# Where in a partition TensorE's streamed operands lie, against its weights: new offsets for two expert layers

## The chip, the core and the metric

One core of one Trainium2 chip runs the whole program. The metric is the device time of one execution in microseconds (us); the kernel before takes 991.43 us (median of 3 runs, 991.33 to 991.97). The engines are TensorE (PE in the rows, its weight loads PEld), VectorE (DVE), ScalarE (ACT), GpSimd (POOL) and SyncE (SP), which issues the DMAs. SBUF is the memory on the chip that operands are read from; it has 128 partitions, and an address here is the byte within a partition. PSUM, in banks of 512 floats per partition, takes the sums of TensorE.

## The reference, cut to what matters

```
x = attention(q, k, v, M_prev, z_prev, beta)      # 4 x 8 heads, 576 tokens of 64, causal, plus a memory term
x = x as [2304 tokens, 512]
h = x @ w_in            # 512 -> 2048
g = s * max(h, 0)**2 + b
x = g @ w_out           # 2048 -> 512          (layer 1)
h = x @ w_in2
g = max(h, 0) + alpha * min(h, 0)
return g @ w_out2       #                      (layer 2)
```

All of it is float32. The two layers hold most of the multiplications.

## The kernel before

**Matmuls of the layers.** A float32 matrix is split in a high and a low part (float32r), and a product is three matmuls: weight high by data high, weight high by data low, weight low by data high (in `g2` the order of the last two differs). Weights are the stationary operand, loaded by 128 x 128; the data is the moving operand, streamed through them, of 512 or 256 columns. Every matmul has its own weight load, which runs while the matmul before it streams.

**Stages.** Layer 1 takes its 2304 tokens in one block of 512 and seven of 256; layer 2 in four of 512 and one of 256 (`BLOCKS`). For each block and each of 16 slices f of the hidden dimension, `g1` (lines 923 to 957) makes 12 matmuls (4 slices d of the model dimension, three each, lines 932 to 934) from X into one PSUM bank; ScalarE and VectorE turn the result into G (layer 1: Relu at line 946, Square at 947, high part at 954, low part at 955; layer 2: lines 949, 952, 954, 955); `g2` (lines 959 to 980) makes 12 matmuls from G (lines 973 to 975) into the output's banks. The g2 of slice f stands behind the g1 of slice f + 1, so that TensorE has work while G is made. In layer 1 block 6 of `BLOCKS` (`ONES`) G has two further columns of ones, so its matmuls in g2 have 258 columns. Layer 1's output is written in halves of two banks (`y_of`, but for the blocks `WIDE`), layer 2's in four banks.

**Order.** `Plan.order` (lines 134 to 283) places all operations on the engines at build time by estimated durations, which depend on the number of columns (`t_r`, line 286), due times and free buffers; addresses don't enter. The attention of batches 0 to 3 is interleaved with layer 1 up to about 423 us of the span; then come the rest of layer 1 (to about 584 us) and layer 2.

**Where operands lie.** Tiles lie in the partition in the order in which they are made (lines 331 to 375, the weights `wt` 0 to 11 behind the last of them), each begun at a multiple of 32 bytes:
- `lead`, 64 bytes; `room` 12 to 15, 8192 bytes each, later the weights `wt` 12 to 15; `pool` 30720 and `poolx` 17920, multiples of 256. `xr2`, the X of layer 2, takes the place of `poolx`.
- `xr`, 16512 bytes (64.5 x 256), the X of layer 1.
- `gr`, 4608 bytes (18 x 256), then `gr2`, 4096: the G of both layers. `gr` has four buffers of 256 columns (2 x lo + j, j alternating with the slices f in layer 1) with a pitch of 1152 bytes (4.5 x 256), or two of 512 columns.
- small tiles (`gt`, `vsc`, `allone`, `mz`, `ident`, `mask` and so on) and `tail`, 96 bytes; together with the half in `xr` they bring `wt` 0 to the residue mod 256 that `room` 12 has (in the built program 2240 and 116928 bytes, both 192 mod 256; `xr` begins at 83648, also 192; `gr` at 100160 and `gr2` at 104768, both 64).
- `cut` (line 353) gives operand number k of n columns; those under 512 columns lie 64 bytes (`HALF`, 16 floats) further. `g_of` (line 907) does the same for `gr2`.

```
x = k * (step or n) + (HALF if n < NBIG else 0)
return t[:, x:x + n]
```

In layer 1 `gj` alternates 0 and 1 (0 for the block of 512), in layer 2 it alternates 0 and 2, where 2 stands for `gr2` (line 941). `xs` says which X buffer a block uses.

Of the kernel before, what the change touches and what calls it, by code (L numbers as in the profile page):

```python
# [6 lines left out]
F32 = mybir.dt.float32  # L7
F32R = mybir.dt.float32r
# [13 lines left out]
NBIG, NB = 512, 256  # L22

SCRATCH = 2048
TAIL = 24
HALF = 16
PITCH = NB + 2 * HALF

WIDE, ONES = (0, 6, 7), 6
KD = DM // 128  # L30
# [284 lines left out]
def build(tc, kp, vd, qp, mzd, beta8, sb2, win1, wout1, win2, wout2, alpha, outT):  # L315
# [8 lines left out]
    with tc.tile_pool(name="sb", bufs=1) as sb, tc.tile_pool(  # L324
        name="ps", bufs=1, space=bass.MemoryType.PSUM
# [2 lines left out]
        y1 = dr.tile([128, KD, NT], F32, name="y1")  # L328


        sb.tile([128, HALF], F32, name="lead")
        room = [sb.tile([128, 3 * GW], F32, name=f"room{f}", tag=f"wt{f}") if f >= KF - XF else None for f in range(KF)]
        made = {}

# [6 lines left out]
        poolx = sb.tile([128, XS * GW], F32, name="poolx", tag="poolx")  # L341

        def xr2():
            if "xr2" not in made:
                made["xr2"] = sb.tile([128, 2 * KD * NBIG + HALF], F32R, name="xr2", tag="poolx")
            return made["xr2"]

        xr_ = sb.tile([128, 4 * KD * NB + 2 * HALF], F32R, name="xr")
        gr_ = sb.tile([128, 4 * PITCH], F32R, name="gr")
        gr2 = sb.tile([128, 2, NBIG], F32R, name="gr2")  # L350
        gt_ = sb.tile([128, 2 * NB], F32, name="gt")

        def cut(t, n, k, step=None):

            x = k * (step or n) + (HALF if n < NBIG else 0)
            return t[:, x:x + n]

        vsc = sb.tile([128, 2, 6], F32, name="vsc")
# [15 lines left out]
        bcs = sb.tile([128, KD], F32, name="bcs")  # L374
        sb.tile([128, TAIL], F32, name="tail")

# [516 lines left out]
        def x_of(n, xs, lo, d):  # L893

            if xs == 2:
                return cut(xr2(), n, KD * lo + d)
            if n == NBIG:
                return cut(xr_, n, KD * lo + d)
            return cut(xr_, n, 2 * KD * xs + KD * lo + d, NB)
# [7 lines left out]
        def g_of(n, lo, j, extra=0):  # L907

            if j == 2:
                x = HALF if n < NBIG else 0  # L910
                return gr2[:, lo, x:x + n]
            if n == NBIG:
                return cut(gr_, n, lo)
            return cut(gr_, n + extra, 2 * lo + j, PITCH)

# [7 lines left out]
        def g1(layer, n, xs, f):  # L923
# [17 lines left out]
            gj = 2 * (cm["g"] % 2) if layer == 2 else 0 if n == NBIG else cm["g"] % 2  # L941
            cm["g"] += 1
            t_, G_h, G_l = t_of(n, gj), g_of(n, 0, gj), g_of(n, 1, gj)
            tk = ("gt", gj)
            if layer == 1:
# [13 lines left out]
        def g2(layer, blk, n, f, gj):  # L959
            extra = 2 if (layer, blk) == (1, ONES) else 0  # L960
            G_h, G_l = g_of(n, 0, gj, extra), g_of(n, 1, gj, extra)
            if f == 0:
                yslot.clear()
                if layer == 1 and blk in WIDE:
                    yslot.update({d: Bank([4 + d]) for d in (2, 3)})
            for d in range(KD):
                yk, Y = y_of(layer, blk, d)

                first = f == 0 and (layer == 2 or blk in WIDE or d % 2 == 0)

                def mm(d=d, Y=Y, first=first):
                    W_h, W_l = (wt(f, 1, lo)[:, d * 128:(d + 1) * 128] for lo in range(2))
                    T.matmul(Y, W_h, G_h, start=first, stop=False, skip_group_check=True)  # L973
                    T.matmul(Y, W_l, G_h, start=False, stop=False, skip_group_check=True)  # L974
                    T.matmul(Y, W_h, G_l, start=False, stop=False, skip_group_check=True)  # L975

                op("PE", 3 * t_r(n), mm, r=wkeys("wo", f) + [("gh", gj), ("gl", gj)],
                   w=[yk, ("g2", f)] + ([(yslot[d], "y")] if d in yslot else []),
                   prio=MOE + cm["m"] + (1.5 if layer == 1 and n == NBIG else 0))
            cm["m"] += 1  # L980

        def ones():


            for j in range(2):
                A.copy(out=g_of(NB, 0, j, 2)[:, NB:], in_=one)
                A.activation(out=g_of(NB, 1, j, 2)[:, NB:], in_=one, func=AF.Copy, scale=0.0)
# [165 lines left out]
```

## Time and profile before

| | |
|---|---|
| median of 3 runs | 991.43 us |
| the profiled execution | 990.51 us |
| its span, first to last instruction | 988.4 us |
| TensorE busy, of the span | 972.3 us (98%) |
| weight loads busy | 832.5 us (84%) |
| VectorE, ScalarE busy | 602.7 us (61%), 470.3 us (48%) |
| granted clock of TensorE, mean | 0.999 |

The profile records each instruction's start and duration. Matmuls overlap in the records, since the end of one is modelled, so the sum of durations says little; how fast TensorE goes is read from the distance of one start to the next. The timeline's starts are in us with two decimals, so that a distance over twelve matmuls is good to about 1 ns each.

### The profile page before, as it was taken

Reading aid. Unit: us, or ns where it says so; the run is one execution under the profiler, and the core shown is the slowest. Engines: PE = TensorE matmul, PEld = TensorE weight load, DVE = VectorE, ACT = ScalarE, POOL = GpSimd, SP = SyncE. Lnnn points to the kernel's source line nnn. Section 1 sums busy time; section 2 is a strip of 40 time slices with the busy share of each in tenths; the row PEclk is TensorE's granted clock in tenths of the full one; section 3 lists DMA queues with packets and bytes.
Section 4 is the critical chain, followed back from the end, with each engine's and each line's share of the span. In section 5 each row is a group of like instructions: output and inputs, shape, how many; then the busy total and the mean of one; then the engine's idle time right before and its main releaser. Section 6 shows DMA issues by size and latency. Waiting matters only on the chain.

```text
span 988.4 us, 18001 instructions
## 1 busy us (share of the span) xinstructions
PE 972.3 (98%) x7068; PEld 832.5 (84%) x7068; DVE 602.7 (61%) x1471; ACT 470.3 (48%) x1183; POOL 5.3 (1%) x29
## 2 busy tenths in 40 slices
PE   7999999999999999999999999999999999999998
PEld 5777777788888888999999998888888888888898
DVE  7999998677776766442122999945334433534354
ACT  7877766787777777644454653212112111211111
POOL 1000000000000000000000000000000000000000
PEclk9999999999999999999999999999999999999999
DMA  5359955475667545451000755402000100100010
GB/s 175 100 167 244 244 180 154 103 165 112 150 129 153 142 107 114 102 173 44 1 23 20 219 163 163 152 1 86 1 1 14 61 1 1 43 1 0 1 44 22
DMA packets 114692, 93.22 MB, mean 94 GB/s; under 512 B 83376, under 2 KB 94640, under 8 KB 114608
## 3 DMA queue, kind: packets, MB, share of 16 engines
q1 hardware_dynamic: 114608, 92.08, 34.6%
q8 instruction: 55, 0.90, 0.4%
q14 instruction: 29, 0.24, 0.1%
HBM read 59.29 MB, written 13.11 MB: 73 GB/s over the span
## 4 chain that ended last, share of the span: by engine, by line
PE 91%; DVE 4%; ACT 4%; issue 1%; DMA 0%; SPq 0%; ACTq 0%
PE yb L973 14%; PE yb L975 13%; PE yb L974 13%; PE hb L932 9%; PE hb L934 8%; PE hb L933 8%; PE sp L933 3%; PE sp L932 3%; PE sp L934 3%; PE ob L775 2%; PE ob L933 2%; PE ob L934 2%; PE ob L932 2%; PE yb L775 2%; PE sp L775 2%; PE sp L679 1%
## 5 line engine op out<-in xcount | busy, mean ns | idle before, releaser
L973 PE MATMUL yb<-gr,wt 128*128 128x256 f32 (+2 forms) x832 | 272.2, 327 | 0.7 <-ACT gr L954 0.5
L975 PE MATMUL yb<-gr,wt 128*128 128x256 f32 (+2 forms) x832 | 270.1, 325 | 0.0
L974 PE MATMUL yb<-gr,wt 128*128 128x256 f32 (+2 forms) x832 | 269.2, 324 | 0.0
L932 PE MATMUL hb<-xr,wt 128*128 128x256 f32 (+1 forms) x592 | 184.3, 311 | 5.3 <-ACT gt L946 3.7
L934 PE MATMUL hb<-xr,wt 128*128 128x256 f32 (+1 forms) x592 | 179.6, 303 | 0.3 <-DVE wt L882 0.3
L933 PE MATMUL hb<-xr,wt 128*128 128x256 f32 (+1 forms) x592 | 179.6, 303 | 0.0
L973 PEld LDWEIGHTS yb<-gr,wt 128*128 128x128 f32 x832 | 156.4, 188 | 18.0 <-issue 2.5
L975 PEld LDWEIGHTS yb<-gr,wt 128*128 128x128 f32 x832 | 156.6, 188 | 15.2 <-DVE gr L955 0.6
L974 PEld LDWEIGHTS yb<-gr,wt 128*128 128x128 f32 x832 | 156.3, 188 | 14.0
L955 DVE TENSOR_TENSOR gr<-gt,gr 128x256 fp32r<-128x256 f32 (+1 forms) x168 | 83.9, 499 | 129.8 <-ACT gr L954 129.1
L954 ACT CAST gr<-gt 128x256 fp32r<-128x256 f32 (+1 forms) x168 | 78.3, 466 | 146.3 <-DVE gt L952 139.1
L932 PEld LDWEIGHTS hb<-xr,wt 128*128 128x128 f32 x592 | 111.2, 188 | 18.5 <-ACT gt L946 5.9
L934 PEld LDWEIGHTS hb<-xr,wt 128*128 128x128 f32 x592 | 111.0, 188 | 6.0 <-DVE wt L882 0.7
L933 PEld LDWEIGHTS hb<-xr,wt 128*128 128x128 f32 x592 | 111.2, 188 | 4.7
L946 ACT ACTIVATE gt<-hb 128x256 f32<-128x256 f32 (+1 forms) x128 | 52.4, 410 | 102.7 <-PE hb L934 102.1
L954 ACT CAST gr<-mz 128x512 fp32r<-128x512 f32 (+1 forms) x40 | 23.1, 578 | 156.3 <-DVE mz L952 153.6
L933 PE MATMUL sp<-xr,wt 128*128 128x512 f32 (+1 forms) x160 | 58.9, 368 | 0.0
L932 PE MATMUL sp<-xr,wt 128*128 128x512 f32 (+1 forms) x160 | 58.9, 368 | 0.0
L934 PE MATMUL sp<-xr,wt 128*128 128x512 f32 (+1 forms) x160 | 58.9, 368 | 0.0
L947 ACT ACTIVATE gt<-gt 128x256 f32<-128x256 f32 (+1 forms) x128 | 56.8, 444 | 2.6
L955 DVE TENSOR_TENSOR gr<-mz,gr 128x512 fp32r<-128x512 f32 (+1 forms) x40 | 25.5, 638 | 25.0 <-ACT gr L954 25.0
L949 DVE TENSOR_SCALAR mz<-ob,alv 128x512 f32<-128x512 f32 (+1 forms) x20 | 13.9, 697 | 38.9 <-PE ob L934 38.9
(343 smaller groups left out, 1481.9 us busy)
## 6 DMA issues: line engine op xcount, KB each, us to landing
pool<-wout SPq DMA_DIRECT2D x18, 512.0 KB, 4.4
pool<-win SPq DMA_DIRECT2D x16, 512.0 KB, 4.3
room<-wout SPq DMA_DIRECT2D x14, 512.0 KB, 3.9
room<-win SPq DMA_DIRECT2D x13, 512.0 KB, 4.2
pool<-y SPq DMA_DIRECT2D x18, 256.0 KB, 4.3
out_t<-pool SPq DMA_DIRECT2D x16, 256.0 KB, 2.1
y<-pool SPq DMA_DIRECT2D x22, 128.0 KB, 1.8
pool<-kp SPq DMA_DIRECT2D x9, 288.0 KB, 4.1
```

The costliest lines, as they stand in the source:

```text
L775: T.matmul(bank_at(bk)[rows, x:x + n], half(sqp, odd, q0, nq), half(sk, odd, k0, n), start=True, stop=True, skip_group_check=True)
L932: T.matmul(H_, W_h, X_h, start=(d == 0), stop=False)
L933: T.matmul(H_, W_h, X_l, start=False, stop=False)
L934: T.matmul(H_, W_l, X_h, start=False, stop=(d == KD - 1))
L946: op("ACT", t_act(n, 50), lambda: A.activation(out=t_, in_=H_, func=AF.Relu), r=[hk, "gr"], w=[tk], prio=-1)
L947: op("ACT", t_act(n), lambda: A.activation(out=t_, in_=t_, func=AF.Square), w=[tk], prio=-1)
L949: op("DVE", t_dve(n, 1.04, 60), lambda: V.tensor_scalar(out=t_, in0=H_, scalar1=0.0, scalar2=alv[:, f:f + 1], op0=ALU.min, op1=ALU.mult), ...
L954: op("ACT", t_act(n), lambda: A.copy(out=G_h, in_=t_), r=[tk], w=[("gh", gj)], prio=-1)
L955: op("DVE", t_dve(n), lambda: V.tensor_tensor(out=G_l, in0=t_, in1=G_h.bitcast(F32), op=ALU.subtract), r=[tk, ("gh", gj)], w=[("gl", gj)], ...
L973: T.matmul(Y, W_h, G_h, start=first, stop=False, skip_group_check=True)
L974: T.matmul(Y, W_l, G_h, start=False, stop=False, skip_group_check=True)
L975: T.matmul(Y, W_h, G_l, start=False, stop=False, skip_group_check=True)
```

## The change

Operands of fewer than 512 columns begin 192 bytes (`SKEW`, 48 floats) further instead of 64; the pitch of the four buffers in `gr` is 1280 bytes (5 x 256) instead of 1152; `xr` has 16640 bytes (65 x 256) instead of 16512, `tail` 224 instead of 96. So `gr` and `gr2` begin at the residue mod 256 of the weights, and `wt` 0 keeps it. `gr2` and the small tiles begin 640 bytes further on, `gr` 128, `wt` 0 to 11 768.

```diff
-TAIL = 24
-HALF = 16
-PITCH = NB + 2 * HALF
+TAIL = 56
+SKEW = 48
+PITCH = 320
...
-        sb.tile([128, HALF], F32, name="lead")
+        sb.tile([128, 16], F32, name="lead")
...
-                made["xr2"] = sb.tile([128, 2 * KD * NBIG + HALF], F32R, name="xr2", tag="poolx")
+                made["xr2"] = sb.tile([128, 2 * KD * NBIG + SKEW], F32R, name="xr2", tag="poolx")
...
-        xr_ = sb.tile([128, 4 * KD * NB + 2 * HALF], F32R, name="xr")
+        xr_ = sb.tile([128, 4 * KD * NB + 64], F32R, name="xr")
...
-            x = k * (step or n) + (HALF if n < NBIG else 0)
+            x = k * (step or n) + (SKEW if n < NBIG else 0)
...
-                x = HALF if n < NBIG else 0
+                x = SKEW if n < NBIG else 0
```

## Rows read from the trace of the kernel before

**Rows 1.** The page: busy time by engine; the costliest group of instructions.
```profile
PE 972.3 (98%) x7068; PEld 832.5 (84%) x7068; DVE 602.7 (61%) x1471; ACT 470.3 (48%) x1183; POOL 5.3 (1%) x29
...
L973 PE MATMUL yb<-gr,wt 128*128 128x256 f32 (+2 forms) x832 | 272.2, 327 | 0.7 <-ACT gr L954 0.5
```

**Rows 2.** The page: the chain of waits that ended last, by engine.
```profile
PE 91%; DVE 4%; ACT 4%; issue 1%; DMA 0%; SPq 0%; ACTq 0%
```

**Rows 3.** Windows: length, busy us and instructions by engine, granted clock, DMA.
```profile
core 0: us, PE busy (x) PEld busy (x) DVE busy (x) ACT busy (x) POOL busy (x), PEclk, DMA share, GB/s
64.00:184.00 120.00, 117.03 (x685) 87.12 (x686) 110.60 (x274) 83.25 (x189) 0.41 (x2) 1.00 0.72 196
184.00:423.00 239.00, 237.80 (x2569) 210.29 (x2569) 161.20 (x512) 181.98 (x509) 2.04 (x10) 1.00 0.57 129
423.00:584.00 161.00, 160.53 (x1378) 159.63 (x1371) 70.73 (x149) 82.41 (x203) 0.00 (x0) 1.00 0.30 94
600.00:900.00 300.00, 300.00 (x1305) 244.51 (x1304) 151.83 (x231) 51.12 (x85) 0.00 (x0) 1.00 0.12 37
```

**Rows 4.** Timeline of TensorE in layer 2 (start, duration, both us): 512 columns.
```profile
723.35 0.40 PE L973 MATMUL yb<-gr,wt 128*128 128x512 f32 x1
...
726.14 0.39 PE L932 MATMUL sp<-xr,wt 128*128 128x512 f32 x1
...
726.84 0.39 PE L932 MATMUL sp<-xr,wt 128*128 128x512 f32 x1
...
728.88 0.40 PE L973 MATMUL yb<-gr,wt 128*128 128x512 f32 x1
```

**Rows 5.** Timeline of TensorE in layer 1: 256 columns, G at 64, X, G at 192.
```profile
471.50 0.28 PE L973 MATMUL yb<-gr,wt 128*128 128x256 f32 x1
...
472.92 0.28 PE L932 MATMUL hb<-xr,wt 128*128 128x256 f32 x1
...
474.33 0.28 PE L973 MATMUL yb<-gr,wt 128*128 128x256 f32 x1
...
474.68 0.28 PE L973 MATMUL yb<-gr,wt 128*128 128x256 f32 x1
...
475.70 0.28 PE L932 MATMUL hb<-xr,wt 128*128 128x256 f32 x1
```

**Rows 6.** Timeline of TensorE in layer 2's last block: 256 columns, G at 192.
```profile
953.08 0.28 PE L973 MATMUL yb<-gr,wt 128*128 128x256 f32 x1
...
954.49 0.28 PE L932 MATMUL sp<-xr,wt 128*128 128x256 f32 x1
```

**Rows 7.** Timeline of TensorE in block ONES: G of 258 columns, X of 256.
```profile
502.84 0.28 PE L973 MATMUL yb<-gr,wt 128*128 128x258 f32 x1
...
504.29 0.28 PE L932 MATMUL hb<-xr,wt 128*128 128x256 f32 x1
...
505.70 0.28 PE L973 MATMUL yb<-gr,wt 128*128 128x258 f32 x1
...
507.13 0.28 PE L932 MATMUL hb<-xr,wt 128*128 128x256 f32 x1
...
508.49 0.28 PE L973 MATMUL yb<-gr,wt 128*128 128x258 f32 x1
```

**Rows 8.** Timeline of TensorE: two G runs at 192 behind a break.
```profile
250.36 0.28 PE L975 MATMUL yb<-gr,wt 128*128 128x256 f32 x1
...
250.70 0.28 PE L975 MATMUL yb<-gr,wt 128*128 128x256 f32 x1
...
423.55 0.28 PE L974 MATMUL yb<-gr,wt 128*128 128x256 f32 x1
...
424.84 0.28 PE L932 MATMUL hb<-xr,wt 128*128 128x256 f32 x1
```

**Rows 9.** Timeline of TensorE: a G run at 192 behind X of 512.
```profile
584.49 0.28 PE L973 MATMUL yb<-gr,wt 128*128 128x256 f32 x1
...
585.17 0.39 PE L932 MATMUL hb<-xr,wt 128*128 128x512 f32 x1
```

## The prediction

> **What bounds the kernel.** First the page's busy shares, then its chain of waits: TensorE is busy for 98% of the span, and 91% of the chain that ended last is its own matmuls [rows 1, 2]. Then the windows by stage: from 184 us on TensorE is busy in 237.80 of 239, 160.53 of 161 and 300 of 300 us, while VectorE and ScalarE have room [rows 3]. Before 184 us it is less clear: 64 to 184 has VectorE at 110.60 of 120. At the clock the windows show 1.00, the 2.4 GHz level, so no clock is to be won back. L973, first to need a new G, stood idle 0.7 us in 832 times [rows 1]. So the end is set by how soon one matmul follows the other, and the durations of the groups do not say that (they overlap); the start times in the timeline do. Everything below comes from differences of starts.
>
> **Offsets.** Call offset the address of the moving operand less that of the weights, mod 256 bytes. All weights (wt) share one residue, since each holds 8192 bytes and every slice of it starts at a multiple of 512. From the tile sizes in the section on the kernel: 512-column X at 0, 512-column G at 128, 256-column X at 64, 256-column G at 192 for even and 64 for odd buffers in layer 1, and 192 always in layer 2 (there gj is 0 or 2). After: 0 for all 512-column operands, 192 for all of 256 (and the 258-column G of block ONES).
>
> **What offsets cost, in rows.** A run is the 12 matmuls of one g1 or g2 call, read from its first start to the next run's first.
> - 512 columns [rows 4]: G at 128, 726.14 - 723.35 = 2.79 us, 232.5 ns each. X at 0, 728.88 - 726.14 = 2.74 us; but its last nine take 728.88 - 726.84 = 2.04 us, 226.7 ns each, so the excess sits in the three right behind the G run. The window 600:900 agrees: 300 us over 1305 less the one or two at its edges is 230.2 ns, the mean of the two runs 230.4 [rows 3].
> - 256 columns [rows 5]: G at 64 1.42 us, X at 64 1.41 us (117.9 ns), G at 192 1.37 us, of which the last nine take 1.02 us, 113.3 ns each. This G run has the same line, banks and waits as that at 64; only the buffer differs.
> - But 192 isn't always fast: layer 2's G at 192 takes 954.49 - 953.08 = 1.41 us [rows 6]. And 64 isn't always slow: X at 64 takes 508.49 - 507.13 = 1.36 us behind a G run at 64 of 258 columns, and 505.70 - 504.29 = 1.41 us behind one at 192 [rows 7]. So there are two steady paces, 113.3 and 117.9 ns, and a run keeps the one it entered.
>
> I read this as the moving stream and the next weight load meeting in memory, the offset setting who waits; what is shown is only the two paces and their dependence on offset and entry.
>
> **Which pace after.** For 512 columns at 0 the trace has one steady pace, 226.7 ns, that each X run reaches after three matmuls. With G at 0 too nothing pushes it out. For 256 at 192 it depends on the entry. Behind a break, seven runs at 192 have at least seven gaps left; five end at 113.3 (the first: 250.70 - 250.36 = 0.34 us in three), two at 117.9 (the last: 424.84 - 423.55 = 1.29 us in eleven) [rows 8]. The one run at 192 that comes straight from 512 columns at 0 ends at 113.3: 585.17 - 584.49 = 0.68 us in six [rows 9]. That is the very entry that layer 2's last block will have. I take four fifths at 113.3, between five of seven and all.
>
> **The sum.** The floor of twelve matmuls is 12 x 226.7 = 2.72 us, or 12 x 113.3 = 1.36 us.
> 1. Layer 2, 512 columns: 4 blocks x 16 = 64 runs each of X and G. G 64 x 0.07 = 4.5, X 64 x 0.02 = 1.3: 5.8 us, all on the path (300 of 300 us busy).
> 2. Layer 1, block 0: 16 runs each, 16 x 0.09 = 1.4 us. They lie among the attention, with VectorE at 92% [rows 3]; I count half, 0.7, with ends 0 and 1.4.
> 3. 256 columns: X 128 runs (7 blocks of layer 1, 1 of layer 2), 8 of them (every second in block ONES) already fast: 120 x 0.055 = 6.6. G at 64: 48 runs x 0.06 = 2.9. G at 192: 64 runs, of which I take 40 slow (layer 2's 16 and half of layer 1's 48) x 0.05 and 24 x 0.01: 2.2. Together 11.7 us. Four fifths: 9.4. In the stage 184:423, some 45% of these runs, attention's own chain would give part back (ScalarE 182 of 239 us busy); I take off a fifth of that share, 0.9. Left 8.5; ends 0 and 11.7.
> 4. 258 columns: G at 64 takes 1.43 us, at 192 1.45 [rows 7]. 8 runs move to 192: +0.2.
> 5. Other tiles behind gr move by 640 bytes, so mz and ident change their residue by 128. By the loops some 260 matmuls of the attention (L528, L573, L663) read them. No row shows them at another residue; the nearest price is that of 128 against 0, 232.5 - 226.7 = 5.8 ns, so -1.5 to +1.5 us. I take 0, as most lie before 184 us.
> 6. ScalarE and VectorE write G and X and read gt, mask and mz at new addresses. Nothing shows a price. TensorE covers it after 184 us; were the cover gone, 1% on VectorE in 64:184 would be 1.1 us. Taken at 0.
> 7. No instruction, DMA, wait or order changes: the planner's costs use column counts alone. PSUM is untouched, and the 768 bytes more per partition move only addresses.
>
> Sum: 5.8 + 0.7 + 8.5 - 0.2 = 14.8 us. The profiled execution took 990.51 us (span 988.4), so 975.7; the median of the runs is 0.92 above it, 991.43, so **976.6**.
>
> **A rule that speaks against it.** The rows show the same line, shape and bank 5% apart by buffer [rows 5]. The Trainium skill says otherwise: "TensorE: Matmul & The Clock Gate" (Step-by-step: what each phase is for) has loading the next weights take no read bandwidth from the running matmul, over two independent ports, and "SBUF — State Buffer" (Who interferes with whom) that TensorE waits on no one. By that rule the sum is 0 and the time 991.4; the trace disagrees where offset alone changes (113.3 against 117.9 ns), yet the equal 1.41 us of [rows 6] keeps it alive as rival B.
>
> **Rivals.**
> - A, the 256-column matmuls enter the pace of 117.9 ns and, with no offset changing any more, stay there. For it: [rows 6], and 117.9 behind the last break. Against: five of seven, and [rows 9]. Then terms 1, 2 and 4 remain, and what is fast now turns slow, 24 G runs x 0.04 and 8 X runs x 0.055, 1.4: 6.5 - 0.2 - 1.4 = 4.9 us, 986.5. Chance 0.25.
> - B, address matters only by way of the order and banks: the G runs at 512 are slow because they change PSUM banks (X stays in one), not by offset. Then 1 and 2 vanish, and with the 256-column pace set by history 3 is near 0: 991.4. For it: G and X at 512 differ in banks as well as offset. Against: [rows 5], where banks don't differ. Chance 0.11.
> - C, slower: 192 is the worse offset when nothing shifts. The 258-column G shows it, 1.45 us against 1.43. Its place is every 256-column run; at 1.45 each (without credit for the two columns less) against 1.415, 1.36, 1.42, 1.41 and 1.37 now: 120 x 0.035 + 8 x 0.09 + 48 x 0.03 + 40 x 0.04 + 24 x 0.08 = 9.9, less the 6.3 of 512 and 258: +3.6, 995.0. It decides from about 1.435 us per run. Against: no 256-column run at 192 has stood there. Chance 0.06.
>
> **Numbers.** The forecast has 0.53, the rest (0.05) are mixtures. Its own range is 972 (all of 1 to 3, with 1.5 of term 5) to 982 (half of term 3). For 8 in 10 it must reach over A, to 989; below, 972.5. A change of 0.2% (2 us) is about what a measurement of this kernel can tell from none. Faster: forecast, A and most mixtures, 0.83; same: B and a little of C, 0.12; slower: 0.05.
>
> **What would show it.** Right: layer 2's runs of 512 all 2.72 us and the window 600:900 counting some 1325 matmuls instead of 1305; 256-column runs of 1.36 us in X as in G, from 423 us to the end of layer 1 and in the last block; idle before L932 and L973 not grown. Wrong: G at 512 still 2.79 us (B); 256-column runs at 1.41 us (A) or over 1.43 (C); or the gain of 184:423 gone into waits of TensorE on ScalarE.

## The result: 1% faster, less than forecast

| | before | after |
|---|---|---|
| median, us (4 runs each) | 991.38 (991.29 to 991.97) | 981.17 (980.85 to 981.50) |
| profiled execution, its span | 990.51, 988.4 | 980.97, 978.9 |
| TensorE busy | 972.3 (98%) | 962.6 (98%) |

The ratio is 0.9896, 95% interval [0.9879, 0.9913]: 10.2 us faster, where 14.8 were forecast. The time lies in the range (972.5 to 989), near the end of the likeliest case's own (972 to 982). No engine has another instruction or another order.

The page of the profile after, beside [rows 1, 2]: busy time by engine, the chain of waits by engine, and the groups that answer to a new G and a new X.

```profile
PE 962.6 (98%) x7068; PEld 828.7 (85%) x7068; DVE 602.4 (62%) x1471; ACT 471.5 (48%) x1183; POOL 5.3 (1%) x29
...
PE 89%; DVE 5%; ACT 4%; issue 1%; DMA 0%; SPq 0%; ACTq 0%; DVEq 0%
...
L973 PE MATMUL yb<-gr,wt 128*128 128x256 f32 (+2 forms) x832 | 270.7, 325 | 0.7 <-ACT gr L954 0.5
...
L932 PE MATMUL hb<-xr,wt 128*128 128x256 f32 (+1 forms) x592 | 183.9, 311 | 5.3 <-ACT gt L946 3.7
```

L932 on the page before:

```profile
L932 PE MATMUL hb<-xr,wt 128*128 128x256 f32 (+1 forms) x592 | 184.3, 311 | 5.3 <-ACT gt L946 3.7
```

TensorE's busy time falls by 9.7 us and the span by 9.5; the idle time in front of L973 and of L932 is that of before, 0.7 and 5.3 us. So the time came out of TensorE's own pace, and no new wait took its place. The windows after, beside [rows 3] (length, busy us and instructions by engine, granted clock, DMA share, GB/s):

```profile
64.00:184.00 120.00, 117.01 (x688) 87.37 (x689) 110.35 (x273) 83.37 (x191) 0.41 (x2) 1.00 0.70 196
184.00:423.00 239.00, 237.77 (x2593) 210.12 (x2592) 161.67 (x513) 182.21 (x508) 2.04 (x10) 1.00 0.57 129
...
600.00:900.00 300.00, 300.00 (x1325) 248.39 (x1325) 151.23 (x229) 51.74 (x86) 0.00 (x0) 1.00 0.11 36
425.00:490.00 65.00, 65.00 (x573) 64.84 (x573) 19.66 (x44) 31.13 (x79) 0.00 (x0) 1.00 0.24 78
552.00:576.00 24.00, 24.00 (x206) 24.00 (x205) 22.64 (x44) 14.72 (x34) 0.00 (x0) 1.00 0.69 199
940.00:970.00 30.00, 30.00 (x257) 30.00 (x256) 14.13 (x33) 4.08 (x10) 0.00 (x0) 1.00 0.00 1
```

600:900 holds the 1325 matmuls that were forecast, 20 more than in [rows 3]. The last three windows hold matmuls of 256 columns alone, so their counts give the pace, the distance from one start to the next; the lower pace is the faster one. 573 in 65 us are 113.4 ns each (layer 1, the end of block 4 and block 5); 206 in 24 us (its block 7) and 257 in 30 us (layer 2's last block) are 117.9 ns each, once the two or three at the edges, which a window cuts, are left off. About half of the 256-column work reached the lower pace, and half did not. The timeline of TensorE after (start, duration, both us) shows each kind:

```profile
448.50 0.28 PE L932 MATMUL hb<-xr,wt 128*128 128x256 f32 x1
448.85 0.34 PE L973 MATMUL yb<-gr,wt 128*128 128x256 f32 x1
449.02 0.28 PE L974 MATMUL yb<-gr,wt 128*128 128x256 f32 x1
449.26 0.38 PE L975 MATMUL yb<-gr,wt 128*128 128x256 f32 x1
...
449.84 0.28 PE L932 MATMUL hb<-xr,wt 128*128 128x256 f32 x1
...
451.20 0.28 PE L973 MATMUL yb<-gr,wt 128*128 128x256 f32 x1
...
541.67 0.39 PE L932 MATMUL sp<-xr,wt 128*128 128x512 f32 x1
...
542.35 0.28 PE L973 MATMUL yb<-gr,wt 128*128 128x256 f32 x1
...
543.77 0.28 PE L932 MATMUL hb<-xr,wt 128*128 128x256 f32 x1
...
719.97 0.39 PE L932 MATMUL sp<-xr,wt 128*128 128x512 f32 x1
...
722.69 0.39 PE L973 MATMUL yb<-gr,wt 128*128 128x512 f32 x1
...
725.41 0.39 PE L932 MATMUL ob<-xr,wt 128*128 128x512 f32 x1
```

- Layer 2, beside [rows 4]: X takes 722.69 - 719.97 = 2.72 us and G 725.41 - 722.69 = 2.72, at 226.7 ns each.
- Block 5 of layer 1: behind a break (448.85 to 449.26, matmuls 170 to 240 ns apart) X takes 451.20 - 449.84 = 1.36 us.
- Block 7: behind three matmuls of 512 columns at 0, G takes 543.77 - 542.35 = 1.42 us, and so it goes on.

**Where the 10 us came from.** For every matmul of the layers, take the distance to the next start less 226.67 ns (512 columns) or 113.33 ns (256 and 258), the excess, and sum it by term. Left out are the breaks: distances over 40 ns above that, and those to a matmul of the attention.

| term of the prediction | before | after | gain | forecast |
|---|---|---|---|---|
| 1, layer 2, 512 columns | 5.59 us | -0.01 | 5.6 | 5.8 |
| 2, layer 1, block 0 | 1.47 | 0.77 | 0.7 | 0.7 |
| 3, 256 columns | 10.69 | 6.54 | 4.2 | 9.4, of which 0.9 is given back |
| 4, G of 258 columns | 1.19 | 1.33 | -0.1 | -0.2 |
| sum | 18.94 | 8.63 | 10.3 | 15.7 |

The span fell by 9.5, so some 0.8 us was given back elsewhere (0.9 forecast). Term 3 by block: 4 and 5 of layer 1 gain 1.4 and 1.3 us, 1 to 3 (among the attention) 0.6, 0.3 and 0.4, the X of ONES 0.4; block 7 loses 0.3, and layer 2's last block gains nothing.

### The profile page after: what moved, and what is told of

It reads as the page before. It is cut to its first block, busy times and chain, and to the rows that moved or that the text cites. A ratio compares the mean times of both kernels' runs of the same rounds, so it can differ in the third digit from the quotient of the medians.

```text
span 978.9 us, 18001 instructions
## 1 busy us (share of the span) xinstructions
PE 962.6 (98%) x7068; PEld 828.7 (85%) x7068; DVE 602.4 (62%) x1471; ACT 471.5 (48%) x1183; POOL 5.3 (1%) x29
## 4 chain that ended last, share of the span: by engine, by line
PE 89%; DVE 5%; ACT 4%; issue 1%; DMA 0%; SPq 0%; ACTq 0%; DVEq 0%
PE yb L973 13%; PE yb L975 13%; PE yb L974 13%; PE hb L932 9%; PE hb L934 8%; PE hb L933 8%; PE sp L932 3%; PE sp L934 3%; PE sp L933 3%; PE ob L775 2%; PE ob L932 2%; PE ob L934 2%; PE ob L933 2%; PE sp L775 2%; PE yb L775 2%; PE sp L679 1%
## 5 line engine op out<-in xcount | busy, mean ns | idle before, releaser
L973 PE MATMUL yb<-gr,wt 128*128 128x256 f32 (+2 forms) x832 | 270.7, 325 | 0.7 <-ACT gr L954 0.5
L974 PE MATMUL yb<-gr,wt 128*128 128x256 f32 (+2 forms) x832 | 267.6, 322 | 0.0
L932 PE MATMUL hb<-xr,wt 128*128 128x256 f32 (+1 forms) x592 | 183.9, 311 | 5.3 <-ACT gt L946 3.7
L933 PE MATMUL hb<-xr,wt 128*128 128x256 f32 (+1 forms) x592 | 179.1, 303 | 0.0
L973 PEld LDWEIGHTS yb<-gr,wt 128*128 128x128 f32 x832 | 156.4, 188 | 17.1 <-issue 2.5
L974 PEld LDWEIGHTS yb<-gr,wt 128*128 128x128 f32 x832 | 156.5, 188 | 12.2
L932 PEld LDWEIGHTS hb<-xr,wt 128*128 128x128 f32 x592 | 111.3, 188 | 18.2 <-ACT gt L946 6.1
L933 PEld LDWEIGHTS hb<-xr,wt 128*128 128x128 f32 x592 | 111.3, 188 | 4.5
L932 PE MATMUL sp<-xr,wt 128*128 128x512 f32 (+1 forms) x160 | 58.8, 367 | 0.0
L933 PE MATMUL sp<-xr,wt 128*128 128x512 f32 (+1 forms) x160 | 58.8, 367 | 0.0
```

The lines of the kernel that those rows point to most:

```text
L932: T.matmul(H_, W_h, X_h, start=(d == 0), stop=False)
L933: T.matmul(H_, W_h, X_l, start=False, stop=False)
```

## Experiments

Times are medians of 4 runs (10 for `e3` and `e4`); ratios are to the kernel before on the same chip, with 95% intervals. The diffs are against the changed kernel. First one half of the change at a time.

**Only the 512-column operands at their new place (`e1`).** The 256-column operands all lie at 64, where X lay before; G at 192 in half of its buffers moves there too.

```diff
-SKEW = 48
+SKEW = 16
```

> All as in the changed kernel, but the 256-column operands at 64 instead of 192, one offset for X and G. Theory (the offset sets which pace a break ends in, and at 64 that is nearly always 117.9 ns): layer 2's 512-column runs stay at 2.72 us, the 256-column runs go to 1.41 us nearly throughout; the 512-column gain of some 5.9 us remains, and the G runs that had 113.3 ns before lose some 1.4: about 987 us. Rival (what helped the 256 columns was that X and G now share one offset, whichever it is): 256-column runs as in the changed kernel, about 981 us.

986.31 us, 0.9956 [0.9941, 0.9971]. Windows of this kernel:

```profile
600.00:900.00 300.00, 300.00 (x1325) 248.47 (x1325) 154.46 (x236) 52.38 (x87) 0.00 (x0) 1.00 0.11 38
940.00:970.00 30.00, 30.00 (x258) 30.00 (x257) 14.25 (x32) 4.46 (x11) 0.00 (x0) 1.00 0.00 1
```

Layer 2 has its 1325 matmuls, so the gain at 512 columns needs nothing of the 256-column part. With all of 256 columns at 64, nearly all stand at 117.8 ns: the sum of the excess is 13.96 us, 5.0 less than before, and the profiled span 4.5 less.

**Only the 256-column operands at theirs (`e2`).** The 512-column G goes back to 128.

```diff
-TAIL = 56
-SKEW = 48
+TAIL = 24
+SKEW, SKEWG = 48, 16
...
-        xr_ = sb.tile([128, 4 * KD * NB + 64], F32R, name="xr")
+        xr_ = sb.tile([128, 4 * KD * NB + 96], F32R, name="xr")
...
-                x = SKEW if n < NBIG else 0
+                x = SKEWG if n < NBIG else 0
...
-            return cut(gr_, n + extra, 2 * lo + j, PITCH)
+            x = (2 * lo + j) * PITCH + SKEWG
+            return gr_[:, x:x + n + extra]
```

> All as in the changed kernel, but the 512-column G back at 128; everything of 256 columns at 192. Theory (the two widths add up): layer 2's G runs go back to 2.79 us and the first three matmuls of its X runs to some 232 ns, 5.3 us given back, the 256-column blocks of layer 1 keep their pace: about 986.5 us. Rival (512 columns gained by something other than the offset of G): layer 2 keeps 2.72 us in both, about 981 us.

985.42 us, 0.9944 [0.9928, 0.9961]. The two halves, 0.0044 and 0.0056, add up to 0.0100 against the 0.0104 of the change. That is in part chance: at 256 and 258 columns `e1` has 1.3 us more excess than the kernel before, and `e2` has 1.7 us less than the kernel after in layer 2's last block. The timeline of TensorE in layer 2 (L974 is L973 here, L933 is L932):

```profile
720.08 0.40 PE L974 MATMUL yb<-gr,wt 128*128 128x512 f32 x1
...
722.87 0.39 PE L933 MATMUL sp<-xr,wt 128*128 128x512 f32 x1
...
725.61 0.40 PE L974 MATMUL yb<-gr,wt 128*128 128x512 f32 x1
```

G takes 2.79 us again and X 2.74, as in [rows 4], with the order and the banks as in the kernel after: the offset is the cause. (The small tiles behind `gr` lie 128 bytes mod 256 from their place in the kernel after, as in the kernel before; no matmul of the layers reads them.) And one thing differed from the kernel after, in the window of the last block:

```profile
940.00:970.00 30.00, 30.00 (x267) 30.00 (x266) 14.66 (x33) 4.54 (x12) 0.00 (x0) 1.00 0.01 2
```

267 instead of 257 matmuls: with G of 512 at 128 ahead of it, this block runs at 113.3 ns, though its own operands lie just as in the kernel after. So what came before picks the pace (here in two entries of two; behind X of 512 at 0 the three entries of `e2` end at 117.9, as in the kernel after).

**Other offsets for 256 columns (`e3`, `e4`, `e6`, `e7`).** One number changes each time: SKEW = 0 (offset 0), 32 (128), 56 (224), 40 (160).

```diff
-SKEW = 48
+SKEW = 0
```

> All as in the changed kernel, but the 256-column operands at 0 too. Theory carried over from 512 columns at 0, which reach one pace from every entry: 256 columns at 0 reach 113.3 ns from every entry, which takes away most of the 7 us that 256 columns still spend above it: about 974.5 us. Rival (width and offset together set the paces, and 0 is no better than 64 for 256 columns): 117.9 ns or more nearly throughout, 987 us or later.

> All as in the changed kernel, but the 256-column operands at 128. Theory carried over from 512 columns at 128 (232.5 ns against 226.7, so 5.8 ns per matmul above the floor): 256 columns at some 119 ns, nearly 3 ns more than their mean in the changed kernel, 2900 of them: about 989 us. Rival (two paces at any offset, breaks choose evenly): as the changed kernel, 981 us.

> The changed kernel with the 256-column operands at 224, half way between 192 (113.3 or 117.9 ns) and 0 (120.0 ns). If what counts is a piece of 64 bytes: as at 192 or worse, 981 to 992 us, with paces between. Rival (finer steps matter, 224 reaches 113.3 ns from every entry): about 975 us.

> The changed kernel with the 256-column operands at 160, half way between 128 (paces of 118.7 and 120.0 ns on average) and 192. If what counts is a piece of 64 bytes: as at 128 or between 128 and 192, 981 to 990 us. Rival (finer steps matter, 160 reaches 113.3 ns from every entry): about 975 us.

| offset of 256 columns | label | median us | ratio | a matmul, last block |
|---|---|---|---|---|
| 0 | `e3` | 991.79 | 1.0011 [1.0002, 1.0021] | 120.0 ns |
| 64 | `e1` | 986.31 | 0.9956 [0.9941, 0.9971] | 117.8 |
| 128 | `e4` | 989.46 | 0.9989 [0.9979, 0.9998] | 120.0 |
| 160 | `e7` | 987.12 | 0.9958 [0.9943, 0.9973] | 118 to 119 |
| 192 | after | 981.17 | 0.9896 [0.9879, 0.9913] | 117.9 (113.3 elsewhere) |
| 224 | `e6` | 987.38 | 0.9960 [0.9945, 0.9974] | 118.2 |

The pace is not the same in every block: in block 5 `e4` stands at 118.6 ns and `e7` at 117.4. The timeline of TensorE in the last block of `e3`:

```profile
953.69 0.28 PE L973 MATMUL yb<-gr,wt 128*128 128x256 f32 x1
...
955.13 0.28 PE L932 MATMUL sp<-xr,wt 128*128 128x256 f32 x1
...
956.57 0.28 PE L973 MATMUL yb<-gr,wt 128*128 128x256 f32 x1
```

1.44 us a run, in X as in G. I had thought that 0 might be best for every width, as it is for 512 columns (974.5 us); that theory fell at once. Layer 2's 512-column matmuls in `e3` stand at 226.7 ns, and still the kernel is no faster than before: the whole gain of 512 columns goes into the 256-column runs. (In `e3` one VectorE operation also comes at another place in the order; TensorE's order is the same.) Only at 192 do whole blocks stand at 113.3 ns (at 64, in `e1`, 6 of 45 breaks lead there, for a run or a few); of the places tried, the best depends on the number of columns.

**Pushing the last blocks out of the higher pace (`e5`).** In ONES every X run behind a G run of 258 columns goes to 113.3 ns. So one G run of block 7 and one of layer 2's last block get two further columns, whose sums nobody reads.

```diff
-            extra = 2 if (layer, blk) == (1, ONES) else 0
+            extra = 2 if (layer, blk) == (1, ONES) or f == 0 and (layer, blk) in ((1, 7), (2, 4)) else 0
...
-                yk, Y = y_of(layer, blk, d)
+                yk, Y = (("Y", d), ybank[d][:, :n + 2]) if extra else y_of(layer, blk, d)
```

> The changed kernel, with 24 of its matmuls two columns wider: the g2 run of slice 0 in the last block of layer 1 and in the last block of layer 2 streams 258 columns instead of 256 (the two more sums are not read). Theory (a pace lasts until something shifts the two streams against each other, and behind a 258-column run at 192 the X runs of block ONES go to 113.3 ns within three matmuls): both blocks, at 117.8 ns throughout in the changed kernel, go to 113.3 ns for the rest of the block; 15 slices of 24 matmuls x 4.5 ns x 2 blocks = 3.2 us less, 0.2 us for the wide runs: about 978 us. Rival (the pace belongs to the block: its banks, its buffers, what the other engines do beside it): both blocks stay at 117.8 ns, the time is that of the changed kernel plus 0.2 us, about 981.3 us.

980.05 us (979.01 to 981.44), 0.9892 [0.9875, 0.9908]: one block followed, the other did not. The timeline of TensorE of `e5`, block 7 and then layer 2's last block:

```profile
541.20 0.39 PE L932 MATMUL sp<-xr,wt 128*128 128x512 f32 x1
...
541.89 0.28 PE L973 MATMUL yb<-gr,wt 128*128 128x256 f32 x1
...
543.30 0.28 PE L932 MATMUL hb<-xr,wt 128*128 128x256 f32 x1
...
931.77 0.28 PE L973 MATMUL yb<-gr,wt 128*128 128x258 f32 x1
...
933.22 0.28 PE L932 MATMUL sp<-xr,wt 128*128 128x256 f32 x1
...
933.58 0.28 PE L932 MATMUL sp<-xr,wt 128*128 128x256 f32 x1
...
934.60 0.28 PE L973 MATMUL yb<-gr,wt 128*128 128x256 f32 x1
...
935.96 0.28 PE L932 MATMUL ob<-xr,wt 128*128 128x256 f32 x1
```

In layer 2 the wide run costs 1.45 us, the three matmuls behind it 0.36, the next nine 934.60 - 933.58 = 1.02 us (113.3 ns), and the block stays there. In block 7 three matmuls of layer 2's X, 512 columns at 0, come in at 541.20, behind the wide run, and the G run behind them takes 1.41 us again.

**The wide run behind the 512-column matmuls (`e9`).** In block 7 it moves from slice 0 to slice 2 (this diff is against `e5`).

```diff
-            extra = 2 if (layer, blk) == (1, ONES) or f == 0 and (layer, blk) in ((1, 7), (2, 4)) else 0
+            extra = 2 if (layer, blk) == (1, ONES) or (layer, blk, f) in ((1, 7, 2), (2, 4, 0)) else 0
```

> As the kernel with 24 wider matmuls, but in layer 1's last block the 258-column run is that of slice 2 instead of slice 0: behind slice 0 stood three 512-column matmuls of layer 2, and behind those the block went on at 117.8 ns. Theory (what shifts the streams last sets the pace, and nothing of 512 columns comes again until the block's end): layer 1's last block goes to 113.3 ns from slice 3 on, some 13 slices x 24 x 4.5 ns = 1.4 us on top of the 1.5 us of layer 2's last block: about 978.2 us. Rival (layer 1's last block holds 117.8 ns for reasons of its own): that block unchanged, about 979.7 us.

979.57 us (978.57 to 980.63), 0.9887 [0.9872, 0.9901], where 978.2 was expected; the profiled execution took 978.57. Windows of `e9` in block 7 and in layer 2's last block:

```profile
552.00:576.00 24.00, 24.00 (x214) 24.00 (x213) 23.30 (x46) 15.17 (x36) 0.00 (x0) 1.00 0.68 210
...
940.00:970.00 30.00, 30.00 (x267) 30.00 (x267) 14.76 (x34) 4.48 (x11) 0.00 (x0) 1.00 0.00 1
```

214 instead of 206, 267 instead of 257: both blocks now stand at 113.3 ns. The timeline of TensorE of `e9` in block 7, before the wide run:

```profile
541.12 0.28 PE L932 MATMUL hb<-xr,wt 128*128 128x256 f32 x1
...
541.80 0.39 PE L932 MATMUL sp<-xr,wt 128*128 128x512 f32 x1
...
542.49 0.28 PE L973 MATMUL yb<-gr,wt 128*128 128x256 f32 x1
...
543.90 0.28 PE L932 MATMUL hb<-xr,wt 128*128 128x256 f32 x1
```

Six matmuls of X take 0.68 us (113.3 ns), three of 512 columns come in, and the G run behind them takes 1.41 us. So three matmuls of 512 columns are enough to leave that pace, and twelve of 258 to enter it. The excess falls to 5.72 us; the time is not told apart from the kernel after by the intervals alone.

**The kernel after again (`e8`, `e11`), and 64 bytes further on (`e10`).** In `e10` every tile moves by 64 bytes, weights included.

```diff
-        sb.tile([128, 16], F32, name="lead")
+        sb.tile([128, 32], F32, name="lead")
```

> The changed kernel itself, beside the others on their chip: about 981.2 us, with the last blocks of both layers at 117.8 ns.

> The changed kernel with the first tile 64 bytes longer, so that weights and operands all lie 64 bytes further and every offset between them is kept. Theory (what counts is the offset between moving operand and weights): paces and time as in the changed kernel, about 981 us. Rival (an address mod 256 counts by itself): the paces of 256 columns change, to 117.8 ns or 120 ns for most, 986 to 992 us, and those of 512 columns may.

> The changed kernel itself, beside the two others on their chip: about 981 us.

980.53 us (980.21 to 982.55), 0.9896 [0.9882, 0.9911] for `e8`; 981.92 (980.35 to 982.46), 0.9908 [0.9893, 0.9922] for `e11`; 981.21 (980.08 to 982.50), 0.9900 [0.9884, 0.9917] for `e10`. The window 425:490 (block 5) in `e8`, `e11` and `e10`:

```profile
425.00:490.00 65.00, 65.00 (x573) 64.84 (x572) 19.76 (x44) 30.80 (x80) 0.00 (x0) 1.00 0.24 78
```

```profile
425.00:490.00 65.00, 65.00 (x560) 64.84 (x559) 19.60 (x44) 30.41 (x78) 0.00 (x0) 1.00 0.24 78
```

```profile
425.00:490.00 65.00, 65.00 (x560) 64.84 (x559) 19.40 (x44) 30.57 (x78) 0.00 (x0) 1.00 0.24 78
```

`e10` stands with `e11`, measured beside it on the same chip, in the pace of every block and in time, and its 256-column operands lie at 192 mod 256, where those of `e3` lay at 120.0 ns: what counts is the distance of the two operands, not either address. And the same kernel draws block 5 at 113.3 ns in one profile and at 117.9 in another. The timeline of `e11` at the break that is shown above for the kernel after:

```profile
448.25 0.34 PE L973 MATMUL yb<-gr,wt 128*128 128x256 f32 x1
448.43 0.28 PE L974 MATMUL yb<-gr,wt 128*128 128x256 f32 x1
448.67 0.38 PE L975 MATMUL yb<-gr,wt 128*128 128x256 f32 x1
...
449.24 0.28 PE L932 MATMUL hb<-xr,wt 128*128 128x256 f32 x1
...
450.65 0.28 PE L973 MATMUL yb<-gr,wt 128*128 128x256 f32 x1
```

The same instructions, whose starts lie as far apart as there to 0.01 us, and behind it X takes 1.41 us instead of 1.36. Block 5 is worth 1.6 us, which would account for most of the 2.3 us over which the single times of this kernel lie (980.2 to 982.5); only three of them have a profile.

**A nudge for block 5 as well (`e12`).** The edit of `e9`, and in slice 1 of block 5 the X run has 258 columns in nine of its twelve matmuls.

```diff
-        def g1(layer, n, xs, f):
+        def g1(layer, n, xs, f, wide=False):
...
-                    X_h, X_l = x_of(n, xs, 0, d), x_of(n, xs, 1, d)
+                    m = n + 2 if wide and d < KD - 1 else n; H_ = bank_of[hk][:, :m]; X_h, X_l = x_of(m, xs, 0, d), x_of(m, xs, 1, d)
...
-                gj = g1(layer, n, xs, f)
+                gj = g1(layer, n, xs, f, (layer, blk, f) == (1, 5, 1))
```

> The kernel with two nudges, and a third: nine of the twelve matmuls of the g1 run of slice 1 in block 5 of layer 1 stream 258 columns (the two further sums are not read). That block stood at 113.3 ns in three profiles of these kernels and at 117.8 ns in two, of the same addresses. Theory (an execution draws the pace of that block at its last break, and a shift of the streams draws it anew, to 113.3 ns as behind the other 258-column runs): block 5 at 113.3 ns from slice 2 on in every execution, 1.5 us less where it had the other pace, 0.1 us for the wide run; the median near 978.5 us and the executions closer together. Rival (a 258-column run of g1 doesn't act as one of g2 does): the block draws as before, or is sent to 117.8 ns, 979 to 981 us.

978.30 us (977.7 to 978.8), 0.9873 [0.9857, 0.9890], the lowest of the study: every one of its times lies below every one of the kernel after. Its windows:

```profile
425.00:490.00 65.00, 65.00 (x573) 64.86 (x572) 19.64 (x44) 30.90 (x79) 0.00 (x0) 1.00 0.23 78
552.00:576.00 24.00, 24.00 (x214) 24.00 (x213) 23.28 (x46) 15.17 (x36) 0.00 (x0) 1.00 0.67 211
600.00:900.00 300.00, 300.00 (x1325) 248.43 (x1324) 150.00 (x227) 50.65 (x84) 0.00 (x0) 1.00 0.11 36
940.00:970.00 30.00, 30.00 (x268) 30.00 (x267) 14.75 (x34) 4.47 (x11) 0.00 (x0) 1.00 0.00 1
```

All three blocks stand at 113.3 ns. The break at 448.9 us still follows the wide run, so one profile can't say whether that run set block 5 or the break was drawn well; block 5 stood at 113.3 ns without it too, in five of seven profiles with 192 (after, `e2`, `e5`, `e8`, `e9`; not `e10`, `e11`). The narrow spread of the four times speaks for the run, but four good draws in a row are no rarity, so that it set block 5 is not shown.

## Why the prediction was right, and where it was off

- **Terms 1, 2 and 4** held: 5.6, 0.7 and -0.1 us against 5.8, 0.7 and -0.2. `e1` and `e2` show the first by itself, in both directions: its excess is 0.1 us in `e1` and 5.5 in `e2`.
- **Term 3** was mis-sized: 4.2 us instead of 9.4. The step that failed is "four fifths at 113.3". Just under half of the 256-column matmuls reached it (block 5 all, 4 nearly all, 1 to 3 a quarter to a half, block 7 and the last block 2 to 6%), so the forecast's own sign, 1.36 us from 423 us to the end of layer 1 and in the last block, failed in those two. The whole of the term was a little large as well: 11.7 us in the forecast, 10.7 in the trace of the kernel before. Two readings stood behind the four fifths. "Five of seven" behind a break became 28 of 45 in the kernel after (24 to 29 of 45 in the other profiles with 192): a draw, somewhat better than even. And [rows 9], one run at 113.3 behind X of 512, was taken for the rule of that entry; with everything at its new place runs behind 512 columns at 0 end at 117.9 in 5 of 5, in each profile of such a kernel. Had I taken 117.9 for that entry, the 64 runs of block 7 and of the last block would have gained nothing.
- **Given back**: about 0.8 us against 0.9; by the same sum 0.3 in `e8` and 0.6 in `e11`. In the profile after, some 0.5 of it lies in the breaks behind the layers' matmuls, most of that in 184:423, and 0.3 in the distances of the attention's own matmuls of L775. The longest waits of TensorE are what they were.
- **Luck**: the time came in under 982 with block 5 at 113.3 ns in the profile. With the other draw, as in `e11`, it would be some 1.6 us longer (an estimate from the excess of that block). And 982, "half of term 3", works out to 980.9 by the forecast's own terms, so that the measured time lies a little beyond it.
- **Terms 5 and 6** at nothing: 64:184 has VectorE busy for 110.35 us against the 110.60 of [rows 3], and TensorE for 117.01 against 117.03. The distances of the matmuls of L528, L573 and L663 add up to 46.9 us before and 47.0 after. Neither term shows a price.
- **Rival A** (the runs enter 117.9 and stay) is what happened to about half of the stages; its price for the whole was right: `e1`, where nearly all stand at 117.8 ns though at 64, took 986.31 us against its 986.5.
- **Rival B** (order and banks, not the address) fell: `e1` to `e4`, `e6` and `e7` keep TensorE's order and banks, change the offset of one width against the kernel after (981.2), and lie between 985.4 and 991.8 us. B's other half, that history sets the pace, is true within an offset. Each matmul here has its weight load, and its distance to the next moves from 113.3 to 120.0 ns with the distance of the two addresses. The Trainium skill, "TensorE: Matmul & The Clock Gate" (Step-by-step: what each phase is for), has the next weights load without taking read bandwidth from the running matmul. The runs don't agree with a reading of it by which the two addresses can't matter; whether it is the load that takes the time they don't show.
- **Rival C** (192 the worse offset) fell: no run of 256 columns at 192 that had settled took more than 1.42 us; of the places tried 0 and 128 are the dear ones, up to 1.44.

That the streams of data and weights meet in the memory stays an argument: the runs show the dependence on the distance, on the width and on the entry, not the place where a matmul waits. Open are also why the run of [rows 9] went to 113.3, what in a break decides the draw, and whether a nudge pays in blocks 1 to 3; it wasn't tried there, as a wide run costs up to 0.1 us and the next break of the attention draws anew.

## What to carry to other kernels

Where TensorE is the bound and the same matmul has two distances of start, compare the addresses of its moving operand and of the weights mod 256 bytes, and try offsets in steps of 64 bytes or less for each width by itself: here the best and the worst place of the 256-column operands lie 1% of the kernel apart. A pace that a run keeps from its entry can be a draw; count all entries of a kind before giving it a share, and never generalise one. Where a long stage sits in the wrong pace, one run of another width can move it, if it stands behind the last disturbance.

## What the runs showed of the hardware that I had not expected

- At offset 192 matmuls of 256 columns have two lasting paces, 113.3 and 117.9 ns. Three matmuls of 512 columns at 0 lead to the higher, G of 512 at 128 led to the lower in `e2`, a run of 258 columns led to the lower (15 of 15 in ONES after), and a break draws: block 5 of one and the same kernel took 1.6 us more in one profile than in two others.
- Of the offsets tried, the best depends on the width: for 512 columns 0 (226.7 ns) and not 128 (232.5), the only two tried; for 256 columns 192 of six, while 0 is the worst for the kernel (120.0 ns, 991.79 us).
- No lasting pace lay below 113.3 ns for 256 columns or 226.7 for 512, both 0.443 ns a column, at a granted clock of 1.00.
